# A fused attention, feed-forward and top-1 expert kernel: the conversion of float64 weights shared out anew between two engines, and two priorities of its scheduler changed

## The chip, the cores and the metric

The kernel runs on one core of a Trainium2 chip, with all its engines: PE (matrix products), DVE (VectorE), ACT (ScalarE), POOL (GpSimd) and SP, whose queue here only starts DMA transfers. The metric is the device time of one execution in microseconds (us); less is better.

## What is computed

Three layers follow one another on 2304 rows (4 sequences of 576) of width 512:

```python
proj = einsum(x, omega); h = proj - sum(x*x)/2; phi = exp(h - max(h)) / sqrt(m)   # x = q, k, scaled
kv, z = k_p^T v, sum(k_p);  attn = (q_p @ kv) / (q_p . z + 1e-6)      # 8 heads of 64, 128 features
h = x @ w_in;  g = h * clip(h + 3, 0, 6) / 6;  x = g @ w_out          # 512 -> 2048 -> 512
e = argmax(x @ w_gate + bias[modality]);  out = gate * relu(x @ w1[e]) @ w2[e]   # 8 experts, 512 -> 1024 -> 512
```

`w_in` and `w_out` come as 64-bit floating-point numbers, and the kernel reads each as two 32-bit words (low, high) and makes float32 of them itself.

## The kernel before, in words

The rows are cut into 9 groups `g` of 256. The feed-forward layer has 16 hidden chunks `c` of 128 for each group; one pair (g, c) is a step. A step has a product with the tile of `w_in` (into PSUM tile `h`), the activation (ACT writes `r<-h,three`, DVE multiplies: `r<-r,h`) and a product with the tile of `w_out` (into `y`). Group 0 takes both weights as whole float32 (`w_full`), with two products of 128x512 and four of 128x256. From group 1 on each operand is split into a high and a low part in a rounded type (`fp32r`), and three cheaper products stand for one: a product with x split into `x` high and low, and the activation into `gh` and `gl`. The function `split` is a copy (ACT, DVE or POOL) and a subtraction (DVE).

The attention feeds the groups. A unit of k (`k_unit`) makes `kv` and `z` of one sequence and a pair of heads; a unit of q (`q_unit`) makes one quarter of a group's x (`x_t[g, pr]`): projection, exponential, the sums with z (`junk,den<-qp,zb`), the scaling of `qp` by `den`, transposes, the product with `kv`, and the split of the result. A unit has two forms: one with three products per tile (hi and lo), and, once all weights are converted and a stacked omega is there (`calm()`, line 641), one with two products (`k.two`), which costs DVE more (`CUSTOM_DVE` with a running minimum, a `qhl` subtraction of 64x512).

The weights are made ready by `conv()` (line 467). `loads()` starts 32 transfers of 512 KB (16 tiles of each weight): the first 8 into places of the pool `wp`, the others into 4 buffers `words`, each of which comes free when its tile is converted (line 474). Three `worker` tasks call `convert` (line 503): ACT multiplies the high word, read as float32, by 2^-112 in place; DVE multiplies that by 2^-126, which leaves the sign alone; DVE then joins the low word shifted right by 29, and the high word shifted left by 3. The result takes a place from `place()` (line 491): one for each pair of tiles up to chunk 14, in the order of the chunks; chunk 15 goes to the buffers `st`. Two `splitter` tasks (line 530) then make the split tiles `w_in_t` and `w_out_t` for the groups from 1 on, as places of `wp` come free (`gone`, line 521); their copy may go to ACT or POOL, the subtraction is DVE's. For group 1 its `w` splits and its four x's must be there.

The order of all work is fixed when the program is built. Every piece is a generator that yields its next operation; `Issue.run` (line 254) keeps a model clock of each engine, takes the operation that could start first, and of those within 0.08 of it the one with the lowest priority number. Priorities (lines 21 to 31): conversion -0.3, loads -0.1, splits `CUT` -0.1, k units -0.4 while weights are still converted, q units `LATE_Q` -0.2 in that time and -0.05 after it, products of steps 0.05, activations -0.8. On the chip each engine works through its own list in that order.

After the 9 groups come the experts: `route` picks an expert for each row (16 products of 128x512 on DVE per group, `junk,l<-st,words`), rows are gathered by expert, and blocks of 256 rows go through 8 chunks of their expert's weights.

All operations are issued through one helper, so nearly all have the line L222.

Of the kernel before, what the change touches and what calls it, by code (L numbers as in the profile page):

```python
# [7 lines left out]

F32 = mybir.dt.float32
F32R = mybir.dt.float32r  # L10
BF16 = mybir.dt.bfloat16
I32 = mybir.dt.int32
AF = mybir.ActivationFunctionType
ALU = mybir.AluOpType
# [3 lines left out]
P = 128  # L18
# [2 lines left out]
FIRST = -1.0  # L21
LOADS = -0.1
CONVERT = -0.3
CUT = -0.1
LATE_K = -0.4, -0.3
LATE_Q = -0.2, -0.05
PRODUCTS = 0.05
ACTIVATIONS = -0.8
OUT = -0.05
# [4 lines left out]
def f32(ap):  # L34
    return ap.bitcast(F32)
# [9 lines left out]
class Issue:  # L45
# [178 lines left out]
    def op(self, e, m, cond=None, **kw):  # L224

        es = [e] if isinstance(e, str) else list(e)
        outs, ins = self.aps(kw)
        g = Gate([(x, ins, outs, self.cost(x, m, kw)) for x in es], cond)
        yield g
        x = es[g.pick]  # L230
        if x == "A" and m == "tensor_copy":
            kw = dict(out=kw["out"], in_=kw["in_"], func=AF.Copy)
            m = "activation"
        if x == "A" and m == "tensor_scalar":
            kw = dict(out=kw["out"], in_=kw["in0"], func=AF.Copy, scale=kw["scalar1"])
            m = "activation"
        self.do(x, m, **kw)
# [63 lines left out]
def favor_ffn_top1_moe_kernel(  # L301
# [18 lines left out]
    N, DM = out.shape  # L320
# [16 lines left out]
    NW = 2 * KF  # L337
    NB = 4
    NW0 = 8
    NR = 6  # L340
    NC = 3
    WC = KF - 1
# [5 lines left out]
    q = Issue(nc)  # L348
# [55 lines left out]
    def ts(o, a, s1, f1, s2=None, f2=None, e="V"):  # L404
        kw = dict(out=o, in0=a, scalar1=s1, scalar2=s2, op0=f1)
        if f2 is not None:
            kw["op1"] = f2
        return op(e, "tensor_scalar", **kw)
# [58 lines left out]
    def conv():  # L467
# [23 lines left out]
        def place(c, which):  # L491

            if c < WC:
                yield Gate(cond=lambda: c in whole if which else len(whole) == c and NW0 - 1 in issued)
                if not which:
                    whole[c] = q.tile(wp, [P, 2, DM], F32, "w", NW)
                return whole[c][:, which, :]
            if len(short) >= 4 and short[-4] not in cut:
                yield Gate(cond=lambda: short[-4] in cut)
            short.append(2 * c + which)  # L500
            return q.tile(ff, [P, DM], F32, "st", 4)

        def convert(j):
            c, which = j // 2, j % 2
            yield Gate(cond=lambda: j in staged)
            t = yield from place(c, which)
            w = staged.pop(j)
            lo_w, hi_w = w[:, :, 0], w[:, :, 1]

            yield from ts(f32(hi_w), f32(hi_w), 2.0 ** -112, ALU.mult, e="A")  # L510

            yield from ts(t, f32(hi_w), 2.0 ** -126, ALU.mult)
            ti = t.bitcast(I32)
            for w_, n, f in ((lo_w, 29, ALU.logical_shift_right), (hi_w, 3, ALU.logical_shift_left)):
                yield from op(
                    "V", "scalar_tensor_tensor", out=ti, in0=w_, scalar=n, in1=ti, op0=f, op1=ALU.bitwise_or
                )
            done.add(j)
            w_full[which, c] = t

# [27 lines left out]
                yield from convert(j)  # L548

        q.add(loads(), LOADS)  # L550
        for k in range(NC):
            q.add(worker(k, NC), CONVERT)
        for k in range(2):
# [236 lines left out]
    def q_unit(k, g, pr, tags):  # L790
# [38 lines left out]
                    )  # L829
        yield from ts(den, den, 1e-6 * M, ALU.add)  # L830
        yield from op("V", "reciprocal", out=den, in_=den)
        if g:
            yield from tt(qp, qp, den.unsqueeze(2).to_broadcast([P, 2 * GT, M]), ALU.mult)
        else:
            for i in range(2 * GT):
                yield from ts(qp[:, i], qp[:, i], den[:, i:i + 1], ALU.mult, e=("V", "A", "P"))
# [621 lines left out]
```

## Time and profile before

| what | value |
|---|---|
| median of 3 runs | 861.58 us (859.24 to 862.17) |
| the profiled execution | 864.53 us, its span 862.8 us |
| PE busy | 800.2 us, 93% of the span |
| DVE busy | 648.7 us, 75% |
| ACT busy | 481.6 us, 56% |
| POOL busy | 93.2 us, 11% |
| HBM read / written | 86.92 MB / 9.87 MB |

The span runs from the first to the last instruction; 1.73 us of the execution lie outside of it. The share of an engine is a mean over stages: which engine is full, and what it waits for, has to be read stage by stage, from the busy time in stretches, the waits and the timeline.

### The profile page before, as it was taken

What the parts mean: (1) busy time and instruction counts of PE and PEld (TensorE: products, weight loads), DVE (VectorE), ACT (ScalarE), POOL (GpSimd) and SP (SyncE); (2) the same over time, 40 slices, a digit from 0 to 9 for tenths busy, and PEclk for the clock granted to TensorE, in tenths of its full rate; (3) what the DMA queues carried; (4) which work ended last, traced back from release to release, by engine and by line L of the source; (5) the groups of instructions that cost most, each with busy time, mean ns of one, the idle gap of its engine ahead of it and who ended that gap; (6) DMA issues with size and microseconds to landing.
All of it is one profiled execution on the core that took longest, in us unless ns stands there. A gap on an engine that the chain in (4) does not pass through costs nothing. (4 is left out here: it accounts for less than half of the span.)

```text
span 862.8 us, 16678 instructions
## 1 busy us (share of the span) xinstructions
PE 800.2 (93%) x5382; PEld 679.9 (79%) x5382; DVE 648.7 (75%) x2210; ACT 481.6 (56%) x1218; POOL 93.2 (11%) x106
## 2 busy tenths in 40 slices
PE   7799974999999999999999999998994999999994
PEld 5566642888888878888878888997893989899994
DVE  2799999877887868888868777477985778767520
ACT  3766534576777557766655463335354666666411
POOL 0072030001000011000000000002022112221000
PEclk9789995899999999999999999999997999999997
DMA  7727732011311212222021100007368998877300
GB/s 184 260 80 249 257 115 68 21 51 47 86 47 48 64 45 59 67 55 81 12 56 34 38 27 1 25 2 202 108 184 275 274 282 271 262 241 207 105 21 19
DMA packets 110066, 97.72 MB, mean 113 GB/s; under 512 B 15247, under 2 KB 91407, under 8 KB 109968
## 3 DMA queue, kind: packets, MB, share of 16 engines
q1 hardware_dynamic: 106272, 86.57, 34.4%
q0 software_dynamic: 3696, 9.98, 3.4%
q8 instruction: 45, 0.74, 0.4%
q14 instruction: 53, 0.43, 0.2%
HBM read 86.92 MB, written 9.87 MB: 112 GB/s over the span
## 5 line engine op out<-in xcount | busy, mean ns | idle before, releaser
L222 PE MATMUL h<-x,w 128*128 128x256 f32 x2616 | 367.7, 290 | 1.3 <-ACT x L222 0.5
L222 PEld LDWEIGHTS h<-x,w 128*128 128x128 f32 x2616 | 346.1, 192 | 23.3 <-issue 7.1
L222 PE MATMUL y<-w,gh 128*128 128x512 f32 x640 | 204.6, 401 | 0.7 <-ACT gh L222 0.7
L222 DVE TENSOR_TENSOR w<-wraw,w 128x512 fp32r<-128x512 f32 x160 | 107.4, 688 | 27.3 <-ACT w L222 23.2
L222 ACT ACTIVATE r<-h,three 128x256 f32<-128x256 f32 x144 | 68.4, 475 | 105.4 <-PE h L222 99.8
L222 PE MATMUL y<-w,gl 128*128 128x512 f32 x320 | 125.4, 392 | 0.1
L222 PEld LDWEIGHTS y<-w,gh 128*128 128x128 f32 x640 | 109.4, 189 | 19.5 <-issue 3.8
L222 ACT ACTIVATE w<-wraw 128x512 fp32r<-128x512 f32 x157 | 96.2, 629 | 36.5 <-DMA wraw<-in_w_dram 26.2
L222 DVE SCALAR_TENSOR_TENSOR junk<-st,words 128x512 bf16<-128x512 f32 x144 | 98.6, 684 | 1.0
L222 DVE SCALAR_TENSOR_TENSOR r<-r,h 128x256 f32<-128x256 f32 x144 | 60.4, 420 | 46.3 <-ACT r L222 43.9
L222 ACT ACTIVATE gh<-r 128x256 fp32r<-128x256 f32 x126 | 52.5, 416 | 63.3 <-PE y L222 56.1
L222 DVE TENSOR_TENSOR gl<-r,gh 128x256 fp32r<-128x256 f32 x128 | 54.4, 425 | 30.1 <-ACT gh L222 19.5
L222 PEld LDWEIGHTS y<-w,gl 128*128 128x128 f32 x320 | 60.1, 188 | 14.8 <-DVE gl L222 1.0
L222 POOL DMA_INDIRECT order<-og,pi x18 | 19.5, 1083 | 446.8 <-DVE pi L222 415.2
L222 ACT ACTIVATE gh<-h 128x256 fp32r<-128x256 f32 x72 | 27.4, 381 | 50.9 <-PE h L222 44.8
L222 DVE SCALAR_TENSOR_TENSOR gl<-h,gh 128x256 fp32r<-128x256 f32 x72 | 30.3, 420 | 25.7 <-ACT gh L222 25.0
L222 ACT ACTIVATE kp<-kp,mx 112x128 f32<-112x128 f32 (+1 forms) x120 | 39.7, 387 | 9.5 <-DVE mx L222 9.4
L222 ACT ACTIVATE qp<-qp,mx 128x128 f32<-128x128 f32 x120 | 41.8, 393 | 0.0
L222 POOL DMA_INDIRECT out_dram<-st,tok x19 | 20.8, 1097 | 178.6 <-ACT st L222 88.9
L222 DVE SCALAR_TENSOR_TENSOR junk<-qp,zb 128x128 bf16<-128x128 f32 (+1 forms) x144 | 37.3, 288 | 0.9
L222 DVE SCALAR_TENSOR_TENSOR w<-words,w 128x512 int32<-128x512 int32 x44 | 30.4, 714 | 0.0
L222 PE MATMUL kp<-om,khl 128*112 128x256 f32 (+1 forms) x135 | 27.5, 300 | 1.1 <-ACT khl L222 0.8
(268 smaller groups left out, 1067.4 us busy)
## 6 DMA issues: line engine op xcount, KB each, us to landing
wraw<-in_w_dram SPq DMA_DIRECT2D x160, 256.0 KB
words<-in_w_in_dram SPq DMA_DIRECT2D x12, 512.0 KB
words<-in_w_out_dram SPq DMA_DIRECT2D x12, 512.0 KB
qraw<-in_qT_dram SPq DMA_DIRECT2D x38, 128.0 KB
kraw<-in_kT_dram SPq DMA_DIRECT2D x42, 112.0 KB
yrows<-st SPq DMA_DIRECT2D x18, 256.0 KB
vraw<-in_v_dram SPq DMA_DIRECT2D x24, 112.0 KB
w<-in_w_in_dram SPq DMA_DIRECT2D x4, 512.0 KB
```

Source lines behind the costliest of these rows:

```text
L222: return getattr(self.eng[e], m)(**kw)
```

## The change

Four things are changed.

- In `convert`, ACT takes the upper half of the low word as a 16-bit integer and turns it into its top three bits as a 32-bit integer (scale 2^-13, bias 2^-14 - 0.5, rounded on writing). DVE joins to it the sign bit, masked from the high word. ACT scales the high word by 2^-112 as before, and DVE joins it shifted left by 3. So ACT has two operations for a tile where it had one, DVE two where it had three, and they alternate: ACT, DVE, ACT, DVE.
- The places for chunks 0 to 14 are taken by a task of their own (`places`), one after another as soon as the first 8 tiles are loading, where each was taken by its converter.
- `CUT` goes from -0.1 to -0.25, `LATE_Q` from (-0.2, -0.05) to (-0.35, -0.05): while weights are converted, q units now come ahead of conversions, and splits just behind these.
- Units of q from group 1 on that have the form with three products scale `qp` by `den` in four operations of 128x128 on whichever of DVE, ACT and POOL the model finds free, where one DVE operation of 128x512 did it.

```diff
-CUT = -0.1
+CUT = -0.25
-LATE_Q = -0.2, -0.05
+LATE_Q = -0.35, -0.05
...
             if c < WC:
-                yield Gate(cond=lambda: c in whole if which else len(whole) == c and NW0 - 1 in issued)
-                if not which:
-                    whole[c] = q.tile(wp, [P, 2, DM], F32, "w", NW)
+                yield Gate(cond=lambda: c in whole)
                 return whole[c][:, which, :]
...
+        def places():
+            yield Gate(cond=lambda: NW0 - 1 in issued)
+            for c in range(WC):
+                if c == NW - NW0 - 3 * n_streams:
+                    yield Gate(cond=lambda: st["early"] == n_streams)
+                whole[c] = q.tile(wp, [P, 2, DM], F32, "w", NW)
...
+            ti = t.bitcast(I32)
+            half = w.rearrange("p n w -> p (n w)").bitcast(U16).rearrange("p (n w) -> p n w", w=4)
+            yield from op(
+                "A", "activation", out=ti, in_=half[:, :, 1], func=AF.Copy, scale=2.0 ** -13, bias=2.0 ** -14 - 0.5
+            )
+            yield from op(
+                "V", "scalar_tensor_tensor", out=ti, in0=hi_w, scalar=-(1 << 31), in1=ti, op0=ALU.bitwise_and, op1=ALU.bitwise_or
+            )
             yield from ts(f32(hi_w), f32(hi_w), 2.0 ** -112, ALU.mult, e="A")
-            yield from ts(t, f32(hi_w), 2.0 ** -126, ALU.mult)
-            ti = t.bitcast(I32)
-            for w_, n, f in ((lo_w, 29, ALU.logical_shift_right), (hi_w, 3, ALU.logical_shift_left)):
-                yield from op(
-                    "V", "scalar_tensor_tensor", out=ti, in0=w_, scalar=n, in1=ti, op0=f, op1=ALU.bitwise_or
-                )
+            yield from op(
+                "V", "scalar_tensor_tensor", out=ti, in0=hi_w, scalar=3, in1=ti,
+                op0=ALU.logical_shift_left, op1=ALU.bitwise_or,
+            )
...
-        if g:
+        if k.two:
             yield from tt(qp, qp, den.unsqueeze(2).to_broadcast([P, 2 * GT, M]), ALU.mult)
```

The lists of all engines come out otherwise from the first conversions on. Three places matter.

PE at the end of group 0, before: the last product of group 0 (`y1_658<-st_1057`) stands three rows ahead of the first row here, and `h0_1434` is the first product of group 1; the `qa` and `qb` products are units of q of group 1.

```order
L222 MATMUL qb_1307<-ident_74,qp1_119 128x128 x4
L222 MATMUL qa_1318<-om_613,qhl_143 128x256 x2
L222 MATMUL qb_1320<-qp1_119,kvb1_132 64x256 x2
L222 MATMUL qb_1345<-om_613,qhl_143 128x256 x2
L222 MATMUL qb_1356<-om_613,qhl_143 128x256 x2
L222 MATMUL qa_1358<-ident_74,qp0_116 128x128 x4
L222 MATMUL qa_1374<-qp0_116,kvb2_133 64x256 x2
L222 MATMUL qa_1395<-om_613,qhl_143 128x256 x2
L222 MATMUL qb_1397<-ident_74,qp1_119 128x128 x4
L222 MATMUL qa_1408<-om_613,qhl_143 128x256 x2
L222 MATMUL qb_1410<-qp1_119,kvb3_134 64x256 x2
L222 MATMUL h0_1434<-x0_1118,w_1005 128x256 x3
```

The same place now; `h_1476` is the first product of group 1 here.

```order
L223 MATMUL h_1444<-x_600,st 128x256
L223 MATMUL y_661<-w,r 128x512
L223 MATMUL y_662<-w,r 128x512
L223 MATMUL h_1476<-x_813,w 128x256 x3
L223 MATMUL h_1476<-x_853,w 128x256 x3
L223 MATMUL h_1476<-x_1046,w 128x256 x3
L223 MATMUL h_1476<-x_1124,w 128x256 x3
L223 MATMUL kp<-om_76,khl 112x256 x6
L223 MATMUL y_661<-st,r 128x512
L223 MATMUL y_662<-st,r 128x512
```

The products of q that stood between the last product of group 0 and the first of group 1 are gone from there: group 1 now begins ahead of the last two products of group 0.

DVE over the same place, before: `r<-r,h_1205` is the last activation of group 0, the `w<-w` are subtractions of weight splits, `x_1118` is the first x of group 1 to be finished, `junk,l` is routing.

```order
L222 SCALAR_TENSOR_TENSOR r<-r,h_1205 128x256
L222 TENSOR_REDUCE mx<-kp 128x2
L222 TENSOR_TENSOR w<-w 128x512 x16
L222 TENSOR_TENSOR w<-st,w 128x512
L222 TENSOR_SCALAR den_120<-den_120 128x4
L222 TENSOR_TENSOR x_1118<-qa,x_1118 128x256
L222 TENSOR_TENSOR w<-st,w 128x512
L222 TENSOR_SCALAR st<-y_658 128x512
L222 RECIPROCAL den_120<-den_120 128x4
L222 TENSOR_TENSOR qhl<-qraw_115,qhl 64x512
L222 TENSOR_TENSOR qp_119<-qp_119,den_120 128x512
L222 SCALAR_TENSOR_TENSOR junk,l<-st,words 128x512
```

DVE now, from the last activation of group 0 (`r<-r,h_1444`) over the first two of group 1; `x_1449` belongs to group 2.

```order
L223 SCALAR_TENSOR_TENSOR r<-r,h_1444 128x256
L223 TENSOR_TENSOR khl<-kraw,khl 128x224
L223 TENSOR_TENSOR w<-w 128x512 x3
L223 SCALAR_TENSOR_TENSOR r<-r,h_1476 128x256
L223 TENSOR_REDUCE mx<-kp 112x4
L223 TENSOR_TENSOR gl<-r,gh 128x256
L223 TENSOR_TENSOR w<-w 128x512 x3
L223 TENSOR_TENSOR x_1449<-qa,x_1449 128x256
L223 TENSOR_TENSOR w<-w 128x512
L223 SCALAR_TENSOR_TENSOR r<-r,h_1522 128x256
```

The block of sixteen subtractions is spread: 22 of the 32 weight splits stand in DVE's list between the first activation of group 0 and the first of group 1 (32 before), and the rest lie between activations of group 1. All four x's of group 1 are finished before the tenth of group 0's sixteen activations.

ACT in the conversions now, within group 0 (`w<-words` is the new operation on the low word, `words<-words` the scaling of the high word, which alone stood there before):

```order
L223 ACTIVATE w<-words 128x512
L223 ACTIVATE x_853<-qb 128x256
L223 ACTIVATE words<-words 128x512
L223 ACTIVATE kp<-kp,mx 112x128 x4
L223 ACTIVATE r<-h_854,three 128x256
L223 ACTIVATE w<-words 128x512 x3
L223 ACTIVATE qhl<-qraw_115 128x256
L223 ACTIVATE words<-words 128x512
```

ACT's list has 32 operations more for conversions in the whole program, 22 of them `w<-words` as here, and 13 scalings of `qp` by `den`; POOL's has 11 such scalings more.

## Rows read from the trace of the kernel before

**Rows 1.** The page: busy shares, and four of its lines of 40 slices.

```profile
PE 800.2 (93%) x5382; PEld 679.9 (79%) x5382; DVE 648.7 (75%) x2210; ACT 481.6 (56%) x1218; POOL 93.2 (11%) x106
...
PE   7799974999999999999999999998994999999994
...
DVE  2799999877887868888868777477985778767520
...
PEclk9789995899999999999999999999997999999997
```

**Rows 2.** Busy time in stretches: length, each engine's busy time, PE's granted clock, DMA.

```profile
56.11:121.76 65.65, 64.12 (x332) 42.78 (x330) 63.89 (x138) 32.70 (x84) 15.31 (x14) 1.00 0.69 218
121.76:156.22 34.46, 16.88 (x65) 10.50 (x65) 32.35 (x107) 17.61 (x41) 0.94 (x1) 0.57 0.19 56
156.22:212.88 56.66, 56.66 (x431) 49.20 (x431) 43.71 (x204) 37.02 (x102) 2.30 (x2) 0.99 0.16 42
212.88:271.17 58.29, 58.29 (x448) 50.73 (x448) 49.01 (x217) 41.58 (x117) 0.00 (x0) 1.00 0.22 60
...
56.11:156.22 100.11, 81.00 (x396) 53.29 (x395) 96.24 (x243) 50.31 (x125) 16.25 (x15) 0.85 0.52 162
```

**Rows 3.** Waits between 121 and 157 us: the longest of PE.

```profile
PE qa L222 <- DVE qhl L222: 12.9, 2, 11.0
```

**Rows 4.** Timeline, DVE and PE about the end of group 0.

```profile
121.76 0.41 DVE L222 SCALAR_TENSOR_TENSOR r<-r,h 128x256 f32<-128x256 f32 x1
...
122.42 10.12 DVE L222 TENSOR_TENSOR w<-w 128x512 fp32r<-128x512 f32 x16
...
134.87 0.69 DVE L222 TENSOR_TENSOR qhl<-qraw,qhl 64x512 fp32r<-64x512 f32 x1
...
135.61 0.80 PE L222 MATMUL qa<-om,qhl 128*128 128x256 f32 x2 [11.02 <-DVE qhl L222]
```

**Rows 5.** DVE's groups from 56.11 to 156.22, shapes apart: count, busy us, mean ns.

```profile
L222 DVE SCALAR_TENSOR_TENSOR w<-words,w 128x512 int32<-128x512 int32 x44 | 30.4, 714 | 0.0
L222 DVE TENSOR_TENSOR w<-w 128x512 fp32r<-128x512 f32 x30 | 20.4, 739 | 0.0
L222 DVE TENSOR_SCALAR w<-words 128x512 f32<-128x512 f32 x21 | 9.5, 458 | 0.9 <-ACT words L222 0.8
L222 DVE SCALAR_TENSOR_TENSOR junk<-st,words 128x512 bf16<-128x512 f32 x12 | 8.2, 687 | 0.1
...
L222 DVE SCALAR_TENSOR_TENSOR junk<-qp,zb 128x128 bf16<-128x128 f32 x16 | 4.6, 310 | 0.1
L222 DVE TENSOR_REDUCE mx<-kp 112x4 f32<-112x512 f32 x5 | 3.4, 678 | 0.0
L222 DVE TENSOR_TENSOR qp<-qp,den 128x512 f32<-128x512 f32 x4 | 2.8, 690 | 0.1
L222 DVE TENSOR_TENSOR qhl<-qraw,qhl 64x512 fp32r<-64x512 f32 x4 | 2.8, 690 | 0.1
...
L222 DVE CUSTOM_DVE_ANT_0 qp<-qp,qa 128x128 f32<-128x128 f32 x8 | 2.0, 284 | 0.1
...
L222 DVE TENSOR_TENSOR x<-qb,x 128x256 fp32r<-128x256 f32 x2 | 0.8, 424 | 0.0
```

**Rows 6.** ACT's groups from 36 to 157, shapes apart.

```profile
L222 ACT ACTIVATE words<-words 128x512 f32<-128x512 f32 x24 | 16.5, 695 | 15.3 <-DMA words<-in_w_out_dram 7.1 <-DMA words<-in_w_in_dram 3.9 <-DVE w L222 2.6
...
L222 ACT ACTIVATE w<-w 128x128 f32<-128x128 f32 x11 | 3.6, 390 | 0.1
```

**Rows 7.** POOL's groups from 36 to 157, shapes apart.

```profile
L222 POOL CAST w<-w 128x512 fp32r<-128x512 f32 x23 | 22.2, 988 | 53.3 <-DVE w L222 50.0 <-PE h L222 2.7 <-issue 0.7
L222 POOL TENSOR_SCALAR w<-w 128x128 f32<-128x128 f32 x5 | 6.0, 1216 | 40.5 <-DVE w L222 40.5
```

**Rows 8.** Timeline, DVE between 110 and 118 us.

```profile
112.60 2.38 DVE L222 TENSOR_TENSOR w<-w 128x512 fp32r<-128x512 f32 x3
```

**Rows 9.** PE's groups from 60 to 120 us, shapes apart.

```profile
L222 PE MATMUL y<-w,r 128*128 128x512 f32 x52 | 24.6, 596 | 0.0
...
L222 PE MATMUL kp<-om,khl 128*112 128x256 f32 x24 | 4.8, 337 | 0.0
```

**Rows 10.** Tile `words` from 60 to 112 us: duration min/median/max ns, first and last start.

```profile
L222 SPq DMA_DIRECT2D words<-in_w_out_dram x10: 328/328/372, 61.3 to 101.1; - x10
```

**Rows 11.** Timeline: one load of `words`, and ACT's wait for it.

```profile
82.58 0.38 SPq L222 DMA_DIRECT2D words<-in_w_in_dram  x1
...
86.98 0.70 ACT L222 ACTIVATE words<-words 128x512 f32<-128x512 f32 x1 [1.31 <-DMA words<-in_w_in_dram]
```

More of the change, by code (lines that the diff above doesn't have):

```diff
@@ L10 @@
 F32R = mybir.dt.float32r
+U16 = mybir.dt.uint16
 BF16 = mybir.dt.bfloat16
@@ L550, in conv @@
         q.add(loads(), LOADS)
+        q.add(places())
         for k in range(NC):
```

## The prediction

> **What bounds the kernel now.** I read the page first, then the busy time by stretches, then the waits and the timeline where PE is not full.
>
> The page [rows 1] shows PE busy for 93% of the span. Its slices are full nearly everywhere, and full at the full granted clock, with four exceptions: the first slices, the sixth and seventh (108 to 151 us, the clock at 5 tenths in the seventh), the change to the experts (the 31st), and the last. The change touches the work up to about 160 us, so the hole in the sixth and seventh is the one to look at. DVE shows 9 tenths in just those slices.
>
> I measure with one stretch: from DVE's first activation product of group 0 (56.11 us) to its first of group 1 (156.22 us), 100.11 us [rows 2]. In its first part, up to the last activation of group 0 at 121.76, both engines are full: DVE 63.89 and PE 64.12 of 65.65 us. In the second part PE is busy for 16.88 of 34.46 us, at a mean granted clock of 0.57 of full, so mostly at the lower of its levels (1.2 of 2.4 GHz), while DVE is busy for 32.35. At the full clock that work would be 16.88 x 0.57 = 9.6 us, so PE's work in the stretch is 64.1 + 9.6 = 74 us of 100: the stretch costs 26 us more than PE needs. After it PE is busy for 56.66 of 56.66 and 58.29 of 58.29 us.
>
> Why PE waits there is in the waits and the timeline. Its longest wait is 11.0 us for DVE's `qhl` [rows 3]. After the last activation of group 0, DVE works through sixteen subtractions of weight splits, 10.12 us, and comes to `qhl` at 134.87; PE's next product starts at 135.61 [rows 4]. The x's of group 1 were queued behind splits on DVE. So the hole is one of order, on an engine that is full, and it can be closed in two ways: less work on DVE, or the q units ahead of the splits. The change does both.
>
> **DVE, part by part** (counts from the two lists, durations from rows 5). In the stretch go away: the 23 multiplications of conversions, 9.5 us for 21 and 0.8 for two more, so 10.3. Twelve routing products (8.2) and ten of 32 splits (10 x 0.68 = 6.8) move behind it. Units of q of group 1 now have the three-product form, so twelve running minima go (3.0 with the four on the other bank), four `qhl` (2.8) and four scalings by `den` (2.8). That is 33.9. Added are four joins of conversions, since DVE counts 51 and not 47 here (4 x 0.71 = 2.8), five reductions (3.4), four `qhl` of half the size (1.7), two casts (0.8, at 0.42 like the x row), ten products with z (10 x 0.31 = 3.1) and small ones (I allow 1.5): 13.3. DVE's 96.24 becomes 76 us (75.6).
>
> How DVE fares beside POOL needs a price of its own. Three subtractions took 2.38 us while POOL was copying [rows 8], where sixteen took 10.12 without it [rows 4], 0.63 each: 0.48 us lost to some two copies, 0.24 for each POOL operation. The stretch had 15 of these [rows 2] and gets at most 31 (20 copies, 11 scalings), so DVE loses 16 x 0.24 = 4 us more: 80 us.
>
> The Trainium skill (SBUF — State Buffer, Who interferes with whom) has a rule that speaks against this part: a VectorE instruction with two SBUF inputs and a GpSimd instruction that reads SBUF take one port pair as a lock, and whoever comes second is blocked for the whole of the other. The measured 0.24 us is far less than a copy's 0.99, so this trace shows the slowing on VectorE's side but not a whole block; the case in which it were whole is priced below.
>
> **ACT.** Its 50.31 us [rows 2] get 24 integer conversions. No row shows a 16-bit input. I take 0.695 us, the row with the same stride and size [rows 6]: 16.7. The bounds are the DVE multiplication of that size, 0.46 [rows 5], and twice the row, 1.39. Added are 13 scalings by `den` at 0.39 (5.1), two more scalings of words (1.4) and about eight exponentials more (3.0), and 1 for the rest: 77.5 us. ACT comes close to full, but does not set the end.
>
> The Trainium skill (ScalarE: Activation LUTs, Rules for kernel authors) says that multiplications and additions belong on VectorE and not on ScalarE. By the duration alone the trace agrees, 0.458 us against 0.695, and by the rule the conversions' part would be a loss of 24 x 0.24 = 6 us; but the row of the stretch has VectorE at 96 and ScalarE at 50 of 100 us, and there the moved work is worth its whole 10.3.
>
> **PE.** Its 74 us get the q units that come forward and the longer form: 18 products at 0.2 [rows 9] are 3.6, sixteen transposes and products of q at the same price 3.2, less two `y` products that now fall behind the border (four halves at 0.47, 1.9). PE: 79 us, the largest of the three.
>
> **What of it lies on the path.** The stretch can't be shorter than 79 us. With one list full it lost 1.5 to 1.8 us of 65.65 to waits on PE and DVE [rows 2]; now PE, DVE and ACT are at 79, 80 and 77, and each conversion changes engine three times and not once. I take three times the loss, 5 us: 84. So 100.1 - 84 = **16 us** are gained.
>
> Before the stretch DVE loses five multiplications and ACT gains about as many operations, in slices where none of the two is full for long [rows 1]: nothing, within 1 us. `places` alone is worth nothing: it takes places that are free already, under cover of the 32 loads. Behind the stretch about 15 us of DVE work arrive (8.2 and 6.8), less some 5 for two units of q of group 2 that were done early. DVE has 56.66 - 43.71 = 13 us free in the next group and 9 in the one after [rows 2], so PE covers it; if it does not fit, it costs PE time. PE's extra products of the three-product form, 13 in the whole program, are counted above. At the change to the experts the lists are the same.
>
> **Sum.** Span 862.8 - 16 = 846.8, execution 848.5. The profiled execution of 864.53 lies 2.95 above the median of 861.58, so I give the time as 861.58 - 16 = 845.5. The range of this case: 840 (no waits, 79 us) to 850 (10 us of waits).
>
> **Rivals.**
>
> *The work comes back in groups 1 and 2* (0.14). DVE would be at 103 of 115 us over the two, and a list so full makes PE wait. For it: DVE's free time there is in short pieces behind ACT. At 3 to 5 us lost, 849 to 851.
>
> *The conversion chain sets the pace* (0.12, and 0.08 for its slower end). Four `words` buffers carry 20 tiles. Before, ten loads of `w_out` (every second one) were issued from 61.3 to 101.1 us [rows 10], so a load every 2.1 us and 8.4 us for a buffer's turn; 4.4 of them are the transfer [rows 11]. The four operations now take 2.8, so a turn is 7.2 us plus four waits w in the lists. Five turns from 60 us on, and two steps of 4.4 us (65.65 / 15) behind the last tile, give 105 + 20w. At w = 1.75 that is the 140 us of the forecast (56 + 84); at 2.2 it costs 9 us more, 854; from w = 2.6 on it passes 156.2 and the kernel is **slower**, 13 us at w = 3.2, 874. For it: ACT and DVE have two or three operations queued when full. Against it: before, w was about 0.35 with DVE full.
>
> *The lock between DVE and POOL is whole* (0.08). If each of the 16 further POOL operations blocks DVE for its 0.99 to 1.22 us [rows 7], DVE loses 17 us and not 4, and the stretch is 76 + 17 + 5 = 98: 859.5, within the measurement's 0.3% or just below. The Trainium skill's page on SBUF would have it so. Against it: 15 such operations in the stretch left DVE's joins at 0.714 us on average, 0.08 above 0.63.
>
> That the change does not do what it says would need the q units not to finish early; the lists place all four x's before the tenth activation of group 0, and only POOL's slow scalings, 1.22 us each, could hold them up, which is in the waits.
>
> **Chances and range.** Forecast 0.58, the rivals 0.14, 0.12, 0.08 and 0.08. About 0.3% is what a measurement of this kernel can tell from no change. Nearly all of the forecast and of the first two rivals is faster by more than that, of the lock about half: faster 0.88, same 0.04, slower 0.08. The range goes from 838.5 (no waits and 2 us before or behind the stretch) to 857, which leaves out the slower chain and half of the lock.
>
> **What would show it.** In the profile after: no 11 us wait of PE for `qhl` near the end of group 0, the granted clock at full through 120 to 160 us; the first activation product of group 1 at about 140 us (56 + 84); DVE, PE and ACT all above nine tenths before it; the next two groups at 57 and 58 us as before; the low-word operation at 0.6 to 0.7 us on ACT; DVE's joins at 0.68 to 0.75. The forecast is wrong if group 1 begins after 150 us, if PE waits on `w<-words` through group 0, if the new operation takes over 1 us, or if the groups after it grow by more than 3 us.

## The result, and the profile after

The changed kernel takes 833.52 us (median of 4 runs, 833.11 to 834.48) where the kernel before took 860.41 beside it (4 runs, 859.20 to 862.17): a ratio of 0.9688, with a 95% interval of 0.9664 to 0.9711. Run once more, beside other runs of before, it gave 0.9657 (0.9628 to 0.9686). So 27 us were gained where 16 were forecast, and 833.5 lies below the range.

The page of the profile after, with the lines that answer to [rows 1]:

```profile
PE 791.0 (95%) x5395; PEld 675.0 (81%) x5395; DVE 630.8 (76%) x2135; ACT 487.1 (58%) x1245; POOL 99.7 (12%) x114
...
PE   7799999999999999999999999998995999999994
...
DVE  3889999888888868878788785667986777777610
...
PEclk9989999999999999999999999999997999999997
```

The hole in PE's sixth and seventh slice is gone, and so is the 5 of its clock there. The same stretches as in [rows 2], from the profile after: up to the first activation product of group 0 (DVE, from 20 us on), from there to its last, from that to the first of group 1, the two together, and groups 1 and 2:

```profile
20.00:49.77 29.77, 23.64 (x184) 16.28 (x182) 22.56 (x77) 26.63 (x84) 6.15 (x9) 0.89 0.62 215
49.77:128.31 78.54, 77.18 (x457) 52.25 (x457) 74.42 (x190) 66.91 (x172) 27.32 (x26) 1.00 0.61 187
128.31:131.39 3.08, 3.08 (x21) 2.48 (x20) 2.69 (x7) 1.79 (x4) 1.11 (x2) 1.00 0.46 156
49.77:131.39 81.62, 80.26 (x475) 54.73 (x475) 77.10 (x195) 68.70 (x176) 28.43 (x27) 1.00 0.60 186
131.39:187.06 55.67, 55.20 (x428) 48.43 (x427) 49.66 (x198) 41.03 (x113) 1.46 (x1) 1.00 0.24 66
187.06:246.95 59.89, 59.89 (x453) 51.96 (x452) 51.48 (x232) 39.35 (x114) 1.18 (x1) 1.00 0.21 58
```

The same start in the profile before, and first a part of it:

```profile
36.00:48.00 12.00, 7.78 (x39) 4.57 (x38) 11.26 (x54) 11.40 (x39) 4.78 (x5) 0.73 0.05 15
...
20.00:56.11 36.11, 29.07 (x206) 19.97 (x205) 28.68 (x86) 27.91 (x87) 11.97 (x14) 0.76 0.52 178
```

Between the two profiled executions (spans 862.8 and 832.8) the 30.0 us divide so: 6.3 before the stretch (56.11 to 49.77), 18.5 in it (100.11 to 81.62), 3.9 in groups 1 to 7 (397.5 to 393.6), 1.4 lost in the last sixteen steps, and 2.7 in the experts (264.9 to 262.3). The last is no gain of the change: three further executions of before's own list in that part took 261.8, 266.5 and 267.0. The 3.9 us in groups 1 to 7 are work and not waits: PE was busy for 395.1 of the 397.5 us before and for 391.2 of the 393.6 now, with some 44 products fewer, while the stretch has 79 more (475 against 396). Three further executions of before's list took 395.2 to 395.8 us there, so 2 to 3 us are the list's.

At the end of group 0, where [rows 3, 4] have sixteen subtractions and a wait of 11 us, all waits of PE that the view lists for the whole stretch are now these (sum, times, longest):

```profile
PE kp L223 <- DVE khl L223: 1.0, 2, 0.6
PE qb L223 <- POOL qp L223: 0.2, 1, 0.2
```

And DVE and PE in the timeline, from the last activation product of group 0 to the first of group 1:

```profile
128.31 0.41 DVE L223 SCALAR_TENSOR_TENSOR r<-r,h 128x256 f32<-128x256 f32 x1
...
129.10 0.55 DVE L223 TENSOR_TENSOR khl<-kraw,khl 128x224 fp32r<-128x224 f32 x1 [0.39 <-ACT khl L223]
...
129.47 0.96 PE L223 MATMUL kp<-om,khl 128*112 128x256 f32 x6
129.58 1.88 DVE L223 TENSOR_TENSOR w<-w 128x512 fp32r<-128x512 f32 x3
...
130.27 1.88 PE L223 MATMUL y<-st,r 128*128 128x512 f32 x4
...
131.39 0.41 DVE L223 SCALAR_TENSOR_TENSOR r<-r,h 128x256 f32<-128x256 f32 x1
```

The groups of the stretch that answer to [rows 5], on DVE:

```profile
L223 DVE SCALAR_TENSOR_TENSOR w<-words,w 128x512 int32<-128x512 int32 x44 | 31.7, 748 | 0.0
L223 DVE TENSOR_TENSOR w<-w 128x512 fp32r<-128x512 f32 x23 | 16.0, 718 | 0.0
```

To [rows 6], on ACT:

```profile
L223 ACT ACTIVATE words<-words 128x512 f32<-128x512 f32 x24 | 16.1, 699 | 4.1 <-DVE w L223 3.2 <-DVE st L223 0.7
L223 ACT ACTIVATE w<-words 128x512 int32<-128x512 uint16 x22 | 14.9, 690 | 0.3
```

And to [rows 7], on POOL:

```profile
L223 POOL CAST w<-w 128x512 fp32r<-128x512 f32 x16 | 16.8, 1089 | 6.6 <-PE h L223 6.6
L223 POOL TENSOR_SCALAR qp<-qp,den 128x128 f32<-128x128 f32 x11 | 11.8, 1078 | 49.4 <-DVE junk L223 14.6 <-PE qb L223 13.3 <-ACT qp L223 12.0
```

DVE's multiplications of conversions are gone, its joins took 748 ns, and the new operation took 690 ns on ACT. POOL's copies took as long as those of the stretch before (1089 against 1094 ns; the 988 of [rows 7] are a mean over 36 to 157 us).

### The profile page after: what moved, and what is told of

Read it like the earlier page. It is cut to its first block, busy times and chain, and to the rows that moved or that the text cites. A ratio compares the mean times of both kernels' runs of the same rounds, so it can differ in the third digit from the quotient of the medians.

```text
span 832.8 us, 16519 instructions
## 1 busy us (share of the span) xinstructions
PE 791.0 (95%) x5395; PEld 675.0 (81%) x5395; DVE 630.8 (76%) x2135; ACT 487.1 (58%) x1245; POOL 99.7 (12%) x114
## 4 chain that ended last, share of the span: by engine, by line
issue 36%; PE 33%; DMA 15%; DVE 8%; ACT 4%; POOL 1%; SPq 1%; POOLq 0%; DVEq 0%; ACTq 0%
PE h L223 14%; PE y L223 9%; DMA wraw<-in_w_dram 5%; DMA order<-og,pi 4%; DVE w L223 4%; PE qa L223 3%; PE qb L223 3%; ACT w L223 2%; PE kv L223 2%; PE kp L223 2%; DMA xr<-yrows,src 1%; DMA kraw<-in_kT_dram 1%; SPq L223 1%; POOL order L223 1%; DMA w<-in_v_dram 1%
## 5 line engine op out<-in xcount | busy, mean ns | idle before, releaser
L223 PEld LDWEIGHTS h<-x,w 128*128 128x128 f32 x2616 | 343.0, 191 | 22.5 <-issue 3.8
L223 ACT ACTIVATE w<-wraw 128x512 fp32r<-128x512 f32 x152 | 91.2, 627 | 29.1 <-DMA wraw<-in_w_dram 25.7
L223 ACT ACTIVATE gh<-r 128x256 fp32r<-128x256 f32 x126 | 52.5, 417 | 80.3 <-PE y L223 75.1
L223 DVE TENSOR_TENSOR gl<-r,gh 128x256 fp32r<-128x256 f32 x128 | 54.3, 424 | 34.4 <-ACT gh L223 22.0
L223 ACT ACTIVATE qp<-qp,mx 128x128 f32<-128x128 f32 x104 | 36.2, 393 | 0.0
L223 PE MATMUL kp<-om,khl 128*112 128x256 f32 (+1 forms) x140 | 29.4, 307 | 1.5 <-DVE khl L223 1.0
```

The lines of the kernel that those rows point to most:

```text
L223: return getattr(self.eng[e], m)(**kw)
```

## The experiments

Theory: the new priority of q closes the hole at the end of group 0, and DVE's relief decides how much of the work that must then go elsewhere comes back in group 1. Rivals: the conversions are the whole gain; or PE covers what arrives behind the border. To tell them apart, parts of the change were done alone or undone.

**The priority alone**: one line in the kernel before.

```diff
-LATE_Q = -0.2, -0.05
+LATE_Q = -0.35, -0.05
```

> The kernel before with the new LATE_Q alone. Theory A (order): units of q ahead of the conversions close the hole of 26 us at the end of group 0, so the stretch from DVE's first activation product of group 0 to that of group 1 falls from 100 to about 82 us. But DVE does all its old work: its list has only 7 of 32 splits in that stretch and 64 us of work in group 1 (43 before), so group 1 grows from 57 to about 66 us; in sum 8 to 10 us gained, some 851. The start stays at 56 us. Theory B (relief): DVE's work is what sets the end and the order only moves it; the gain of the stretch comes back whole, 858 to 862.

**The conversion alone**: the kernel before with the change's hunk in `convert`.

```diff
-            yield from ts(t, f32(hi_w), 2.0 ** -126, ALU.mult)
...
+                "A", "activation", out=ti, in_=half[:, :, 1], func=AF.Copy, scale=2.0 ** -13, bias=2.0 ** -14 - 0.5
```

> The kernel before with the new conversion alone. Theory A (order): the hole stays, since two x's of group 1 still wait behind all 32 splits; the stretch is 95 to 100 us. Theory B (relief): DVE's list of the stretch goes from 97 to 88 us and the stretch follows it, 90 to 92 us. On the start: if the 6.3 us gained ahead of the stretch come from the conversion's new list, the first activation product is at 50 us here too; if they come with the priorities, at 56. With the start at 50: A 852 to 855, B 844 to 848.

**All but the conversion**: the same hunk undone in the changed kernel.

> The changed kernel with the old conversion (ACT once, DVE three times). Theory A (order): stretch about 82 us, but DVE's list of group 1 is 58 us, so that group takes about 60 and not 56; start at 56; 846 to 850. Theory B (relief): most of the gain is the conversion's, and this kernel is at 855 or above.

**All but the priorities**: the changed kernel with the two lines of numbers of before.

```diff
-CUT = -0.25
+CUT = -0.1
-LATE_Q = -0.35, -0.05
+LATE_Q = -0.2, -0.05
```

> The changed kernel with the old CUT and LATE_Q (new conversion, places, scaling by den on three engines). Theory A (order): two x's of group 1 still wait behind the splits, the hole stays in part, stretch 92 to 96 us; start at 50; 848 to 852. Theory B (relief): DVE's list of the stretch is 85 us, and with start at 50 the whole gain of the change but 3 us is there, 836 to 840.

**Without the places at once**, and **without the scaling in four**, each undone alone in the changed kernel.

```diff
-        q.add(places())
```

> The changed kernel without the task that takes the float32 places at once: each converter takes its own, as before. The list then has 14 splits ahead of group 1 where the changed kernel has 23, and by the durations measured DVE has 58 us of work between the first activation products of groups 1 and 2 where it had 49. A (the places matter only through that order): start 49.8 and stretch 81 to 83 as in the changed kernel, group 1 at 58 to 61 us where it was 55.7, 836 to 839 us. B (PE covers the splits behind the border, as I had predicted of such work): group 1 at 55.5 to 56.5, 833 to 834.5.

```diff
-        if k.two:
+        if g:
             yield from tt(qp, qp, den.unsqueeze(2).to_broadcast([P, 2 * GT, M]), ALU.mult)
```

> The changed kernel with the scaling of qp by den as one DVE operation of 128x512 again. 17 splits stand ahead of group 1 (23 in the changed kernel), DVE's work between the first activation products of groups 1 and 2 comes to 57 us (49). A (DVE is what the stretch and group 1 hang on, so the relief counts): stretch 82 to 84, group 1 at 57 to 60, 835.5 to 840 us. B (POOL and ACT take the scalings where DVE had room): as the changed kernel, 833 to 834.5.

**Conversion and priority**, and **priority and places**, in the kernel before.

> The kernel before with the new conversion and the new priorities of q, without the places at once and the scaling in four. 13 splits stand ahead of group 1 (23 in the whole change, 7 with the priorities alone). A (the priorities close the hole at the end of group 0, and what DVE can't hold there comes back in group 1; the conversion's relief shows in group 1 and in the start): start 50 to 51, stretch 80 to 83, group 1 at 64 to 66 us (72 with the priorities alone, 55.7 in the whole change), 842 to 846 us. B (conversion and priorities are the whole gain): group 1 at 56 to 58, 833 to 837.

> The kernel before with the new priorities and the places taken at once, old conversion. 15 splits stand ahead of group 1 where the priorities alone leave 7, since a splitter may only start when all fifteen places are taken. A (the places count, because they let splits start some 40 us earlier and fill DVE's gaps in group 0): start 54 to 56, first split in the stretch before 75 us (at 110 without), group 1 at 64 to 67 us (72 with the priorities alone), 845 to 849 us. B (the places are worth nothing, as I had predicted): group 1 at 71 to 73, 851 to 853.

Measured (us; start is the first activation product of group 0; splits are the 128x512 subtractions `w<-w` that run within the stretch, one over its border counted; DVE is its busy time in stretch and group 1 together):

| kernel | ratio to before (interval) | start | stretch | group 1 | splits | DVE |
|---|---|---|---|---|---|---|
| before | 1 | 56.1 | 100.1 | 56.7 | 30 | 140.0 |
| lateq_only | 0.989 (0.985 to 0.994) | 55.0 | 80.3 | 72.1 | 7 | 140.8 |
| conv_only | 0.985 (0.981 to 0.989) | 50.6 | 91.5 | 54.4 | 30 | 133.0 |
| lateq_places | 0.984 (0.979 to 0.988) | 54.8 | 82.2 | 64.3 | 13 | 135.9 |
| conv_lateq | 0.981 (0.979 to 0.984) | 49.9 | 81.0 | 65.5 | 13 | 134.5 |
| all_but_conv | 0.984 (0.980 to 0.988) | 54.3 | 82.5 | 65.4 | 12 | 135.0 |
| no_places | 0.979 (0.976 to 0.981) | 49.7 | 83.5 | 65.1 | 14 | 132.3 |
| no_den | 0.976 (0.974 to 0.978) | 50.4 | 80.6 | 63.5 | 17 | 133.4 |
| all_but_prio | 0.998 (0.995 to 1.001) | 50.4 | 93.5 | 55.7 | 30 | 128.2 |
| after | 0.969 (0.966 to 0.971) | 49.8 | 81.6 | 55.7 | 23 | 126.8 |

Three things follow. **The hole is the priority's.** Every kernel with the new `LATE_Q` has a stretch of 80 to 84 us, with the old conversion too; every one without it has 91 or more. Conversion alone makes the hole shorter, and PE's longest wait in its stretch is still for q:

```profile
PE qa L223 <- DVE qp L223: 10.3, 2, 9.5
```

**What doesn't fit comes back in group 1.** With the priority alone only 7 splits stand in the stretch, and group 1 grows by 15 us, with DVE busy for 92% of it and PE waiting, its clock falling to 0.88. The stretch and group 1 of that run:

```profile
55.02:135.28 80.26, 78.88 (x457) 53.37 (x456) 74.53 (x203) 46.59 (x129) 9.42 (x12) 1.00 0.60 188
135.28:207.35 72.07, 63.34 (x468) 54.19 (x467) 66.26 (x234) 44.07 (x121) 6.31 (x8) 0.88 0.21 61
```

And PE's longest waits in its group 1:

```profile
PE kv L222 <- ACT kp L222: 3.6, 3, 2.0
PE kp L222 <- DVE mx L222: 2.4, 2, 1.3
PE kp L222 <- DVE khl L222: 2.4, 3, 0.8
```

In group 1 of the six kernels that have the priority but not the whole change PE is idle for 3.2 to 8.7 us, more than half of it in waits for DVE's `khl` and `mx`, and its mean granted clock is 0.88 to 0.97; in the changed kernel it is idle for 0.5 us, at 1.00. Undoing any one of conversion, places and scaling puts group 1 back to 63.5 to 65.4 us: that is what they are worth there.

In all kernels with the priority, stretch and group 1 together are as long as DVE's work in them divided by 0.89 to 0.93 (after: 126.8 of 137.3, 0.92; lateq_only: 140.8 of 152.3, 0.92). By itself this does not show which engine sets the length: before has 0.89 too and conv_only 0.91, and in the changed kernel PE is busy for 135.5 of the 137.3 us. So the rival of work that comes back was real; the change escapes it since its relief is large enough, and only as a whole. The expectations of group 1 for no_places (58 to 61) and no_den (57 to 60) had the direction and were 4 us short. `CUT` was changed or undone only together with other parts, so its own share is not separated.

**The places count through a condition.** A splitter waits for `len(whole) == WC`, so no split could begin before the last of the fifteen places was taken. The first subtraction of a split, without the task (DVE's timeline of no_places):

```profile
109.82 0.76 DVE L223 TENSOR_TENSOR w<-w 128x512 fp32r<-128x512 f32 x1
```

And with it (after), one just ahead of the stretch and the first that begins in it:

```profile
49.16 0.68 DVE L223 TENSOR_TENSOR w<-w 128x512 fp32r<-128x512 f32 x1
...
61.75 0.68 DVE L223 TENSOR_TENSOR w<-w 128x512 fp32r<-128x512 f32 x1
```

all_but_prio missed both theories: its stretch took 93.5 us, and groups 3 and 5 took 7 us more than in conv_only (64.2 and 69.1 against 62.6 and 64.0). PE waits for q there (2.2 us for DVE's `qp`, 1.6 for `qhl`); why that list fits worse in groups behind the change stays open.

**The start.** The forecast's failed term was tested by the new conversion of the first eight tiles alone, then by holding the clock with the old lists: products whose result is overwritten fill PE's pauses.

```diff
+            if j < NW0:
+                yield from op(
+                    "A", "activation", out=ti, in_=half[:, :, 1], func=AF.Copy, scale=2.0 ** -13, bias=2.0 ** -14 - 0.5
+                )
```

> The kernel before with the new conversion for the first eight tiles alone. A (the earlier start is these tiles' DVE multiplications and the clock): first activation product at 50 to 52 us where it was 56.1; but the hole at the end of group 0 is still there and the q units still stand behind the splits, and the list has 6 us more DVE work ahead of group 1, so the stretch is 102 to 107 us, and the time 858 to 863 us. B (what is gained at the start is kept): stretch 100, 855 to 856. C (the start is not the conversions'): first product at 55.5 to 56.5, 860 to 863.

```diff
+            if k.whole and pr == 0 and i == 1:
+                nxt = bank(banks[1], [P, 1, 2 * M], banks[2])
+                for _ in range(5):
+                    nc.tensor.matmul(out=nxt[:, 0], lhsT=om_f[:, 0:P], rhs=om_f, start=True, stop=True)
```

> The kernel before with five products of 128x256 (0.26 us each at the full clock) put into PE's list in the pause at 22 us, ahead of the kv product that waits for ACT; their result is overwritten, nothing else is moved. A (part of the earlier start is the clock, and the clock falls because of that pause): PE's granted clock stays at full from 25 to 34 us, where it was 0.5, so some 9.5 us of products at half the clock become shorter by up to 4.7 us; the first activation product of group 0 comes 2 to 4.5 us earlier than 56.1, all behind it as before, 857 to 859.5 us. B (the start hangs on the lists of DVE and ACT, the clock is by the way): the clock may be full, but the first activation product stays at 55.5 to 56.5 us, 861 to 862. C (the pause is not what lets the clock fall): 0.5 between 25 and 34 us as before, 861.5 to 863.

The same with two products at the first pause, and with five, each with eight more at the second; then the changed kernel once more, as it is:

> The kernel before with its lists as they are, and the two pauses ahead of the stretch filled by products of the right size: two of 128x256 (0.9 us) at 22 us and eight (3.6 us) at the pause of 4.15 us. What is left between its first activation product and the 48.2 us of the changed kernel with its pauses filled is then the share of the lists, what is gone of 56.1 that of the clock. A (both count, about evenly): full clock from 25 to 48 us, first product at 51 to 52.5 us, stretch 100 to 101, 854.5 to 857 us. B (the clock alone): 48 to 50 us, 852 to 854. C (the second pause's clock is hidden behind DVE and ACT): 52.5 to 53.5, 856 to 858.

> The kernel before with five products at 22 us, with which the clock stayed full up to 40 us (two were too few), and eight at the second pause, 4.15 us long. What stays between its first activation product and the changed kernel's (49.8, 48.9) is then the lists' share. A (clock and lists, about evenly): full clock from 25 to 48 us, first product at 51 to 53 us, 854 to 857.5 us. B (the clock alone): 48.5 to 50.5 us, 852 to 854. C (the clock differs from one execution to the next and the fill doesn't hold it): 55 to 57 us, 860 to 863.

> The changed kernel once more, on the same chip as the two with filled pauses, to compare with. 832.5 to 834.5 us; first activation product at 49.5 to 50.5 us, with the clock at full from 25 to 35 us if that state of the clock belongs to the kernel (A), and at half for part of it if it came about by chance in the first profile (B; then 51.5 to 53 us).

Measured, from 20 us to the first activation product (length, then PE, PE's weight loads, DVE, ACT, POOL, the granted clock), in start_only:

```profile
20.00:50.93 30.93, 24.82 (x185) 17.31 (x184) 22.77 (x78) 27.27 (x84) 7.88 (x12) 0.83 0.61 208
```

In before_fill:

```profile
20.00:53.04 33.04, 25.90 (x214) 18.33 (x213) 28.54 (x87) 27.50 (x87) 11.94 (x14) 0.95 0.57 195
```

In before_fill2:

```profile
20.00:56.41 36.41, 30.91 (x212) 21.71 (x212) 27.99 (x87) 26.29 (x84) 11.57 (x14) 0.81 0.51 177
```

In before_fill5:

```profile
20.00:55.05 35.05, 30.90 (x218) 21.88 (x218) 28.00 (x86) 25.78 (x84) 11.57 (x14) 0.85 0.52 182
```

In lateq_only, with the old conversion and no fill:

```profile
20.00:55.02 35.02, 26.39 (x204) 18.23 (x203) 28.70 (x86) 27.56 (x86) 11.97 (x14) 0.85 0.54 185
```

And in after_again:

```profile
20.00:48.90 28.90, 23.97 (x187) 16.59 (x185) 22.54 (x77) 25.94 (x83) 6.15 (x9) 0.88 0.63 219
```

With the new conversion of the first tiles DVE has 22.5 to 22.8 us to do ahead of the start, with the old one 28.0 to 28.7. Of the 6.1 us between before and after, nine multiplications are 4.3, and 2.3 are four joins that now come behind the first activation product. With DVE's 28 us, a clock that was full from 25 to 40 us brought the start to 53.0 and 55.1 us, so clock alone is worth some 1 to 3 of 56.1 and never came below 53; with the new conversion it was 48.2 to 50.9 in every profile, whether the clock fell or not. Kernels with about the same mean clock from 20 us to the start show the conversion's share alone: at 0.85 with the old one the start came at 54.3 to 55.1 us (lateq_only, lateq_places, all_but_conv, before_fill5), at 0.83 with the new one at 49.8 to 50.9 (start_only, conv_only, conv_lateq, all_but_prio, after_tail). So some 4 to 5 of the 6.3 us are the conversion, the rest goes with the clock. How its share divides between DVE's shorter list and the 20 or so products fewer that PE has ahead of the start (184 in after, 206 before) was not separated. Two products were too few: PE still waited 1.98 us for ACT behind them, and the clock fell.

start_only's total missed: 870.34 us, 1.0% slower (interval 0.7 to 1.3). Its start came as expected, but the stretch took 109.0 where 102 to 107 were expected: the q units still stood last, and PE waited 13.1 us for `qp` where it had waited for `qhl`. before_fill gave 0.9932 (0.9914 to 0.9951), before_fill2 0.9991 (0.9967 to 1.0015), before_fill5 0.9956 (0.9932 to 0.9979).

**A held clock in the changed kernel.** Products in its second pause, then in both places where the clock still falls:

```diff
+        if g == 0 and pr == 0:
+            for _ in range(12):
+                nc.tensor.matmul(out=ps[:, 0], lhsT=om_f[:, 0:P], rhs=om_f, start=True, stop=True)
```

> The changed kernel with products put into its second pause before the stretch: twelve of 128x256 at 34.5 us, where PE waited 3.07 us, and four at 38.5 us, where it waited 1.28; results overwritten. A (the pauses let the clock fall at 39.6, and PE sets the start): the granted clock stays full from 40 to 46 us, six us of products at half become three, the first activation product comes 2 to 3 us earlier than 49.8, 830.5 to 831.5 us. B (DVE and ACT, both full from 34 to 42 us, set the start): full clock but not over 1 us gained, 832.5 to 833.5. C: the clock falls all the same, 833.5 to 834.5.

> The changed kernel with PE's pauses filled in three places, now sized by the measured 0.445 us of a 128x256 product in float32 and 0.13 us in the rounded type: six products (2.7 us) at 34.5 us where PE waited 3.07, two (0.9 us) at 38.5 where it waited 1.28, and 70 of the rounded type (9.3 us) at the change to the experts, where PE waited 7.97 and 2.34 us for gathered rows and the 36 products behind the wait took 6.29 us at half the clock. A (the clock that falls in these pauses costs what the products behind them lose): full clock from 40 to 46 us and behind the change, first activation product at 48 to 48.8 us (49.8), some 3 us less behind the change: 828 to 830.5 us. B (DVE, ACT and the gathers set the time behind both pauses): full clock, but 832.5 to 834.

> The changed kernel with the pauses before the stretch filled as in the run with three fills (six and two products), and the 70 products of the change to the experts put directly ahead of the first transposes of gathered rows, where in that run they stood four rows earlier, ahead of the last products of group 8, and delayed those. A (the clock that falls in a pause costs what the products behind it lose): first activation product at 48.2 us as in that run, the last sixteen steps at 44 to 46 us again, full clock behind the change and the tail 2.5 to 3.5 us shorter than 262.3: span 827.5 to 829.5, some 828.5 to 831 us by the clock of the device. B (the gathers set the time behind the change): full clock, tail 261.5 to 263, 831.5 to 833.

In after_fill the clock stayed full, but a product took 0.445 us and not 0.26, so the fill was too long; first product at 49.7, 0.969 (0.967 to 0.971). In the other two the 70 products went to the wrong block, whose pause it is not, and held PE up at 563 to 576 us, in group 8: 0.973 (0.970 to 0.976) and 0.971 (0.968 to 0.973). At the right place:

> The changed kernel with 80 products of the rounded type (0.118 us each as measured in the last two, 9.4 us) put into the pause at the change to the experts, ahead of the third block's transposes, which is the place where PE waits; in the last two runs they stood at the first block's, 50 us earlier, where PE was busy. A (the clock that falls in the pause costs what the products behind it lose): full clock behind the pause, the 36 products there in 4 us where they took 6.3, tail 257.5 to 260 us (262.3 and 261.5), 829.5 to 831.5 us. B (gathers and the experts' weights set the time behind it): full clock, tail 261 to 263, 832 to 834.

> The same with the pauses before the stretch filled as well (six and two products). A: first activation product at 48.2 to 49 us, tail as in the other run, 828.5 to 831 us. B (the pauses before the stretch are not worth filling, since their length differs from one execution to the next by more than the clock costs): as the other run within 1 us.

after_tail gave 0.9665 (0.9632 to 0.9698), after_fills3 0.9662 (0.9629 to 0.9694), beside 0.9657 of the changed kernel itself: nothing. PE's timeline about the change to the experts in after:

```profile
632.50 0.45 PE L223 MATMUL kp<-ident,xr 128*128 128x128 f32 x1 [7.97 <-DMA xr<-yrows,src]
635.29 0.90 PE L223 MATMUL kp<-ident,xr 128*128 128x128 f32 x3 [2.34 <-DMA xr<-yrows,src]
...
636.70 6.29 PE L223 MATMUL h<-x,w 128*128 128x256 f32 x36
```

And in after_tail:

```profile
624.04 9.75 PE L1155 MATMUL kp<-om 128*128 128x256 f32 x80
633.63 0.27 PE L223 MATMUL kp<-ident,xr 128*128 128x128 f32 x1
635.06 0.55 PE L223 MATMUL kp<-ident,xr 128*128 128x128 f32 x3 [1.15 <-DMA xr<-yrows,src]
...
636.08 2.46 PE L223 MATMUL h<-x,w 128*128 128x256 f32 x10
638.80 3.38 PE L223 MATMUL h<-x,w 128*128 128x256 f32 x26 [0.27 <-DVE x L223]
```

The first four transposes take 0.82 us where they took 1.35, but the rows arrive at 635 us all the same, and the 36 products behind them end 6.1 us after they began where they took 6.3, with a wait for DVE's `x` in between. From the last activation product of group 8 to the end it is 262.2 us where it was 262.3. Theory B holds. No version beat the changed kernel.

## Why the prediction was right and wrong

**Right: the place and the mechanism.** The 11 us wait is gone, the clock is full from 120 to 160 us, the stretch is bound by PE with 80.3 us (79 forecast), and the next groups took 55.7 and 59.9 us (57 and 58 forecast). The low-word operation took 690 ns (695 taken), the joins 748 (680 to 750 named). The lists' counts held nearly: some ten splits and twelve routing products were to leave the stretch; nine splits stand in group 1 and one ahead of the stretch (at 49.16 us, which "The change" overlooks), and 11 routing products in group 1. The first activation product of group 1 came at 131.4 us where 140 was named, 6.3 us of it from the start and the rest from the waits, and ACT was at 0.84 of the stretch and not above nine tenths.

**Wrong: "nothing, within 1 us" before the stretch.** 6.3 us were gained there, the largest part of the error. The step failed by its view: [rows 1] shows averages over 21.6 us, of which it was read that no engine is full for long. The row of the start before shows what should have been asked for: DVE busy for 28.7 of 36.1 us, and for 11.3 of the 12 us from 36 to 48, ACT for 11.4 of them. The new conversion of the first eight tiles alone brought the start to 50.9 us, a held clock with the old one to 53.0 at best. ACT then spends 9.7 us on conversions ahead of the start where it spent 7.9, and the start is still earlier, so ACT's load alone did not hold it; that DVE's did is the likely reading, but no run takes work from DVE there and leaves PE's list as it was.

**Wrong in size: the waits.** "Three times the loss, 5 us" were allowed; PE was idle for 1.4 of 81.6 us (81.62 less 80.26). That made the stretch 18.5 us shorter and not 16. DVE had 77.1 us (80 forecast) and ACT 68.7 (77.5), so neither was as full as the allowance supposed, and each conversion's three changes of engine cost nothing that PE felt.

**Left out: the groups behind.** The forecast put 6.8 us of PE work into the stretch for q units that come forward and for their longer form, and took nothing off the groups behind; they had 3.9 us less to do.

**Right for the whole, wrong as a rule: "PE covers it".** What arrives in group 1 was covered in the changed kernel, but the half changes show that it is so by DVE's relief: DVE's 13 us of free time in group 1 took up 9 subtractions and 11 routing products, but not the 25 and 16 that lateq_only has there.

**Wrong: "`places` alone is worth nothing".** The condition `len(whole) == WC` was not read. Without the task group 1 takes 9.4 us more, and the ratio is 0.979 where the whole change has 0.969.

**The chain of conversions** (`words`) didn't set the pace: none of PE's waits in the stretch is for a converted tile. Its price was read slightly wrong (ten `w_out` loads from 61.3 to 101.1 us are a load every 2.2 us, not 2.1). In the changed kernel they were issued from 63.5 to 116.6 us, a load every 2.95 and 11.8 us for a buffer's turn, so the waits w were about 1.2 us, below the 1.75 that the rival needed. **The lock between DVE and POOL** is not whole: POOL had 27 operations in the stretch against 15, and the joins went from 714 to 748 ns, which is 44 x 0.034 = 1.5 us, less than the 4 allowed. In the changed kernel's stretch the 27 joins that ran beside no POOL operation took 0.68 us, the 20 beside one 0.83 on average and 1.10 at most. The rule of the Trainium skill (SBUF — State Buffer, Who interferes with whom), by which the second is blocked for the whole of the first, would by an estimate have cost 12 further POOL operations of 1.08 us, 13 us; the run does not show that. **ScalarE for arithmetic**: the Trainium skill's advice (ScalarE: Activation LUTs, Rules for kernel authors) to leave multiplications and additions to VectorE is right on one operation, 690 ns against 458. By it the hunk would be left out, and that run exists: all_but_conv has 8.2 us more DVE work in stretch and group 1 (135.0 against 126.8), PE waits 3.5 us for DVE's `khl` and `mx` in that group, and its ratio is 0.984 against 0.969.

## What to carry to other kernels

When a list is reordered so that late work comes first, ask at once what becomes late in its place, and add up the full engine's work over the stretch and its successor together: here that sum over 0.92 gave stretch and successor of every variant with the new order within 4%, and that of the kernel before too, so it tells the length and not the cause. Before a stretch is costed at nothing, ask for the busy time in windows as short as the stretch itself, since slices of 21.6 us hide 12 us of a full engine. And read the conditions under which work may start, not only its priority: a task that "only takes what is free" let other work begin 60 us earlier.

## What the runs showed of the hardware

The granted clock is not a property of the program alone. Behind a pause of PE of 1.79 us it stayed full from 25 to 35 us in after, and behind one of 0.58 us in after_again; in after_tail, which has the same list up to there, the pause was 1.04 us, and the clock was 0.71 (half, 1.2 of 2.4 GHz, for part of the time) from 25 to 30 us:

```profile
25.00:30.00 5.00, 5.00 (x56) 3.42 (x55) 2.48 (x7) 4.72 (x18) 0.00 (x0) 0.71 1.07 377
```

Its first activation product came at 49.76 us all the same, as in after (49.77). Products that hold the clock up bought nothing in the changed kernel (0.9665 and 0.9662 with them, 0.9657 without), and between nothing and 0.7% in the kernel before. ACT's conversion from 16-bit to 32-bit integers, with three of four 16-bit elements skipped, took 690 ns for 128x512, no more than its float32 scaling of every second 32-bit word (699).
